# Larger weight loads (18 in place of 22) and three wider transposing matmuls in a single-core decode kernel

## The chip, the cores and the metric

The kernel runs on one core of a Trainium2 chip. The metric is the device time of one execution in microseconds (us). A kernel is run several times, with the kernel before on the same chip beside it; I quote medians. The ratios quoted are the mean time of one kernel's fast runs over that of the other's fast runs of the same rounds, so they are not quite the ratio of the medians; their 95% interval is given in brackets. "Fast" is a label that the measurement gives each run; on one core it marks a run as slow when it lies more than 1.5% above the fastest of the same kernel.

## The reference, cut to what matters

One decode step of a transformer block, batch 2, one token, width 640. There are 32 heads of 192; the last 1,024 rows of the key and value caches count. Everything is bf16.

```python
mod = (silu(c) @ w_mod)                                     # six modulation rows
h = layernorm(x) * (1 + ca) + sa
q = h @ wq                                                  # 640 -> 6144
o = softmax(q k^T * 192**-0.5) v                            # k, v: last 1024 rows of the caches
x = x + ga * (o @ wo)                                       # 6144 -> 640
h = layernorm(x) * (1 + cb) + sb
x = x + gb * ((gelu(h @ w_gate) * (h @ w_up)) @ w_down)     # 640 -> 1536 -> 640
```

Every weight and cache row is read once, 76.88 MB in all, and there are only two tokens to use it on.

## The kernel before

All loads of weights and caches go out from one engine (SP) on one queue, in a fixed order: w_mod, wq, keys and values of batch 0 and 1 interleaved, wo, w_gate, w_up, w_down. They share one arena in the on-chip memory. A load is issued when the tiles that lay in its place have been read. Each load has its own semaphore, so a consumer waits for a whole load, not for the rows that it needs first.

```python
K_SPLIT = [[(0, 64), (64, 64), (128, 128)], [(0, 128), (128, 128)]]   # 5 loads
V_SPLIT = [[(0, 128), (128, 128)], [(0, 128), (128, 128)]]            # 4
WQ_SPLIT = [(0, 2), (2, 3)]                                           # 2
WO_SPLIT = [(0, 28), (28, 17), (45, 3)]                               # 3
WU_SPLIT = [(0, 3), (3, 2)]                                           # 2
WD_SPLIT = [(9, 3), (0, 5), (5, 3), (8, 1)]                           # 4; w_mod and w_gate: one each
# ... cut
def pump(*consumed):                     # issue the next loads whose place is free
    queue["done"].update(consumed)
    while queue["next"] < len(items):
        # ... cut: stop at the first load whose place is still in use
        queue["ops"][it] = S.dma("sp", k_dma(view(it), source(it)), sem_of[it], writes=keys(it), ...)
# ... cut: wo, one group of matmuls for each load
for ci, (t0, n) in enumerate(WO_SPLIT):
    # ... 2 n matmuls, four at a time in four quarters of the array
    S.op("pe", f, reads=keys(("wo", ci)) + ["oT"], ...)
# ... cut: second layer norm, w_gate, gelu, w_up, product aR
def a_T(e):                              # aR (rows in four quarters) to columns
    for i in range(NR):                  # NR = 4
        for r in range(FR):              # FR = 3
            c0 = 2 * (i * FR + r)
            last = e.matmul(ps[:, 2, c0:c0 + B], lhsT=aR[...][:, :, r], rhs=selg[:, i, :], start=True, stop=True)
# ... cut: w_down, one group of matmuls for each load; last product, sum, store
```

## Time and profile before

| | before |
|---|---|
| time, median of 3 runs | 186.31 us (186.27 to 186.47) |
| load queue's share of the 16 DMA engines' span | 97.2% |
| first row moves, last row of w_down has moved | 1.00 us, 181.68 us |
| VectorE busy, TensorE busy | 58%, 58% |

First the DMA lines of the page: the busy share of the 16 DMA engines in 40 slices of the span in tenths, and the load queue with its packets, its MB and its share of the engines' span.

```profile
DMA  9989999999898989999998989899999999999990
...
q1 hardware_dynamic: 3180, 76.88, 97.2%
```

Nines and eights from the first slice to the last but one: the DMA engines never rest. The chain that ended last (start in us, length in us, what) says the same from the other end:

```profile
...
155.23 26.50 DMA arena<-in_B_w_down_dram
181.73 0.04 issue
181.77 0.74 PE ps L690 x16
182.51 0.02 issue
182.54 0.34 DVE fin L695
182.87 0.02 issue
182.89 0.33 DVE finb L697
```

The end of the kernel hangs on w_down's last rows, and then needs 3.3 us: matmuls, two steps on VectorE, and the store. Now the places that the change touches, from the timeline (start, length, engine, line, operation, count; in brackets the idle time before the first of them and what ended it):

```profile
...
21.57 2.73 PE L478 MATMUL ps<-arena,hT 128*2 128x512 bf16 x24 [0.98 <-DVE opc L464]
32.43 4.01 PE L478 MATMUL ps<-arena,hT 128*2 128x512 bf16 x36 [8.13 <-DMA arena<-in_A_wq_dram]
...
40.91 5.09 DVE L504 TENSOR_TENSOR arena<-arena,qbc 128x3072 bf16<-128x3072 bf16 x3 [3.73 <-DMA arena<-in_A_k_cache_dram]
...
62.66 1.76 DVE L504 TENSOR_TENSOR arena<-arena,qbc 128x3072 bf16<-128x3072 bf16 x1 [2.78 <-DMA arena<-in_A_k_cache_dram]
...
160.68 2.08 PE L627 MATMUL ps<-arena,oT 128*2 128x512 bf16 x56 [0.42 <-DMA arena<-in_A_wo_dram]
167.01 1.89 PE L627 MATMUL ps<-arena,oT 128*2 128x512 bf16 x40 [4.25 <-DMA arena<-in_A_wo_dram]
...
174.73 3.64 PE L661 MATMUL ps<-arena,h2T 128*2 128x384 bf16 x40 [0.27 <-DVE h2T L441]
179.11 0.47 PE L678 MATMUL ps<-selg,aR 128*128 128x2 bf16 x12 [0.74 <-DVE aR L670]
...
181.77 0.71 PE L690 MATMUL ps<-arena,aT 128*17 128x160 bf16 x16 [0.62 <-DMA arena<-in_B_w_down_dram]
```

L478 is the wq product: 24 matmuls on the first load, 36 when the second has landed. L504 is the key multiply on VectorE (DVE): it waits for its first key load at 40.91 us and for the third at 62.66 us. L627 is wo, L661 w_gate and w_up, L678 the transpose, L690 w_down.

The trace also has one record for each piece that a DMA engine moves (a row of one partition). Sixteen engines share 128 rows, so a load is eight pieces and one semaphore write on each engine. Mean durations in the kernel before:

```
piece bytes   count   mean ns   16 engines, GB/s
        4       356         9     (semaphore writes)
     1280       128        55     372
     3840       384       152     406
    24576       384       914     430
    49152       896      1821     432
```

### The profile page before, as it was taken

The numbers are of one execution on the slowest core, as the hardware profiler recorded it, in microseconds if no ns is written. First come the engines' busy times: TensorE is split into PE (matmuls) and PEld (weight loads), VectorE is DVE, ScalarE is ACT, GpSimd is POOL, SyncE is SP. The second block draws the span as 40 slices with busy tenths as digits, with TensorE's granted clock in tenths as the row PEclk, the third lists the DMA queues.
The fourth block names the chain that finished last, engine by engine and source line by source line (L and its number), as shares of the span: only waits on it lengthen the run. The fifth ranks groups of instructions, "written<-read, shape, count | busy, mean of one in ns | idle before, by whom it ended". The sixth has DMA issues, their size and how long they took to land.

```text
span 185.0 us, 1611 instructions
## 1 busy us (share of the span) xinstructions
PE 107.2 (58%) x835; PEld 28.5 (15%) x558; DVE 106.7 (58%) x99; ACT 14.5 (8%) x27; POOL 6.5 (4%) x27
## 2 busy tenths in 40 slices
PE   0015720857766379662499565966662499715472
PEld 0011100040000000001252000600001266401231
DVE  6213000119699488965991999789975938202411
ACT  2032100140000000001000000010001000101610
POOL 7600000000000000000000000000000000000000
PEclk9999995555799966998559999999999569996576
DMA  9989999999898989999998989899999999999990
GB/s 324 449 376 436 462 446 404 434 425 494 377 489 361 510 361 489 436 414 457 395 461 383 478 383 489 383 468 436 418 446 404 442 403 449 398 414 426 406 383 34
DMA packets 3202, 76.97 MB, mean 416 GB/s; under 512 B 378, under 2 KB 508, under 8 KB 1148
## 3 DMA queue, kind: packets, MB, share of 16 engines
q1 hardware_dynamic: 3180, 76.88, 97.2%
q8 instruction: 5, 0.08, 0.2%
q10 hardware_dynamic: 16, 0.01, 0.0%
q14 instruction: 1, 0.01, 0.0%
HBM read 76.88 MB, written 0.00 MB: 416 GB/s over the span
## 4 chain that ended last, share of the span: by engine, by line
DMA 57%; DVE 24%; PE 16%; ACT 1%; issue 1%; SPq 1%
DMA arena<-in_A_k_cache_dram 35%; DMA arena<-in_B_w_down_dram 14%; DVE arena L504 14%; PE ps L567 9%; DMA arena<-in_w_mod_dram 8%; DVE S_sb L523 6%; PE ps L516 3%; DVE Em L553 2%; PE ps L456 2%; DVE negm L533 1%; ACT E_sb L541 1%; SPq L283 1%; PE ps L544 1%; PE ps L537 1%; DVE M L529 0%
## 5 line engine op out<-in xcount | busy, mean ns | idle before, releaser
L516 PE MATMUL ps<-arena,ident_b 128*128 128x512 bf16 x192 | 51.3, 412 | 25.8 <-DVE arena L504 25.8
L504 DVE TENSOR_TENSOR arena<-arena,qbc 128x3072 bf16<-128x3072 bf16 x32 | 54.8, 1750 | 8.3 <-DMA arena<-in_A_k_cache_dram 8.3
L567 PE MATMUL ps<-arena,Em 128*64 128x384 bf16 x256 | 26.6, 379 | 5.7 <-DVE Em L553 5.7
L523 DVE TENSOR_REDUCE S_sb<-ps 128x32 f32<-128x1024 f32 x16 | 19.5, 1218 | 10.1 <-PE ps L516 10.1
L567 PEld LDWEIGHTS ps<-arena,Em 128*64 128x64 bf16 x256 | 16.4, 128 | 31.0 <-DVE Em L553 22.2
L553 DVE TENSOR_TENSOR Em<-E_sb,maskE 128x2048 bf16<-128x2048 bf16 x8 | 18.0, 2283 | 3.4 <-PE ps L567 3.4
L478 PE MATMUL ps<-arena,hT 128*2 128x512 bf16 x60 | 6.7, 625 | 9.1 <-DMA arena<-in_A_wq_dram 8.1
L531 PEld LDWEIGHTS ps<-ident_f,M 128*1 128x1 f32 x2 | 0.2, 80 | 60.5 <-DVE M L529 60.5
L488 DVE CAST qrow<-ps 128x512 bf16<-128x512 f32 x1 | 0.7, 692 | 15.0 <-PE ps L478 15.0
L627 PE MATMUL ps<-arena,oT 128*2 128x512 bf16 (+1 forms) x96 | 4.0, 312 | 4.7 <-DMA arena<-in_A_wo_dram 4.7
L635 DVE COPY arena<-ps 128x128 f32<-128x128 f32 x1 | 0.3, 292 | 10.5 <-PE ps L627 10.5
L541 ACT ACTIVATE E_sb<-S_sb,nbias 128x256 bf16<-128x256 f32 x2 | 1.0, 508 | 65.8 <-DVE nbias L539 65.8
L574 ACT ACTIVATE On<-ps,rden 128x384 bf16<-128x384 f32 x2 | 1.2, 580 | 49.5 <-PE ps L567 49.5
L397 PE MATMUL ps<-ident_b,crow 2*128 2x2 bf16 x5 | 0.4, 177 | 7.9 <-DMA crow<-in_c_dram 7.9
L456 PE MATMUL ps<-arena,scT 128*17 128x480 bf16 x40 | 4.3, 597 | 0.7 <-DMA arena<-in_w_mod_dram 0.7
L410 PE MATMUL ps<-st,selstat 128*128 128x2 f32 x4 | 1.1, 348 | 6.1 <-ACT sqj L406 6.1
L402 DVE CAST X<-xr 128x160 f32<-128x160 bf16 x1 | 0.2, 245 | 6.4 <-DMA xr<-in_A_x_dram 6.4
L661 PE MATMUL ps<-arena,h2T 128*2 128x384 bf16 x40 | 3.6, 507 | 0.3 <-DVE h2T L441 0.3
L494 PE MATMUL ps<-qrow,selq 128*128 128x192 bf16 x16 | 2.7, 361 | 1.2 <-ACT qrow L485 1.2
L464 DVE TENSOR_SCALAR opc<-modR 128x160 f32<-128x160 f32 x2 | 0.5, 244 | 4.7 <-ACT modR L461 4.7
L437 PE MATMUL ps<-selrow,hrow 128*32 128x2 bf16 x40 | 0.7, 182 | 3.6 <-DVE hrow L428 3.6
L478 PEld LDWEIGHTS ps<-arena,hT 128*2 128x2 bf16 x20 | 0.6, 107 | 14.3 <-DMA arena<-in_A_wq_dram 9.9
(84 smaller groups left out, 52.8 us busy)
## 6 DMA issues: line engine op xcount, KB each, us to landing
arena<-in_A_v_cache_dram SPq DMA_DIRECT2D x4, 6144.0 KB, 25.8
arena<-in_A_k_cache_dram SPq DMA_DIRECT2D x3, 6144.0 KB, 39.2
arena<-in_A_k_cache_dram SPq DMA_DIRECT2D x2, 3072.0 KB, 42.5
arena<-in_w_mod_dram SPq DMA_DIRECT2D x1, 4800.0 KB, 14.2
arena<-in_A_wq_dram SPq DMA_DIRECT2D x1, 4608.0 KB, 31.2
arena<-in_A_wo_dram SPq DMA_DIRECT2D x1, 4480.0 KB, 25.8
arena<-in_A_wq_dram SPq DMA_DIRECT2D x1, 3072.0 KB, 20.7
arena<-in_A_wo_dram SPq DMA_DIRECT2D x1, 2720.0 KB, 31.9
```

The lines of the kernel that those rows point to most:

```text
L283: return lambda e: e.dma_start(dst, src)
L456: last = e.matmul(ps[32 * i:32 * i + RM, half, 0:MH].rearrange("p (m n) -> p m n", n=DR), lhsT=scT[:, k, :], rhs=wv[:, 3 * half:3 * half + ...
L478: last = e.matmul(ps[32 * i:32 * i + B, n, :], lhsT=hT[:, k, :], rhs=wv[:, kk, i, n * QW:(n + 1) * QW], start=(k == 0), stop=(k == KT - 1) ...
L494: last = e.matmul(ps[:, BK_T + b, 0:Dh], lhsT=selq[:, b, u * P:(u + 1) * P], rhs=qrow[:, u * Dh:(u + 1) * Dh], start=(u == 0), stop=(u == ...
L504: S.op("dve", lambda e: e.tensor_tensor(out=kt, in0=kt, in1=qbc[:, b, :].unsqueeze(1).broadcast_to([P, JC, Dh]), op=ALU.mult), reads=[("qb ...
L516: last = e.matmul(o_ap, lhsT=ident_b[:, :], rhs=kt[:, :, t * GC:(t + 1) * GC], start=(t == 0), stop=(t == NCH - 1))
L523: S.op("dve", lambda e: e.tensor_reduce(out=S_sb[:, b, 2 * JC * pair:2 * JC * (pair + 1)], in_=ps[:, 2 * z:2 * z + 2, :].rearrange("p k (j ...
L541: S.op("act", lambda e: e.activation(out=E_sb[:, b, :], in_=S_sb[:, b, :], func=ACTF.Exp, scale=SCALE, bias=nbias[:, b:b + 1], accum_out=d ...
L553: S.op("dve", lambda e, z=z, j=j: e.tensor_tensor(out=Em[:, z, :, :], in0=E_sb[:, b, j:j + JE].unsqueeze(2).broadcast_to([P, JE, H]), in1= ...
L567: last = e.matmul(ps[64 * i:64 * i + 2 * H, BK_O, 0:ON], lhsT=Em[:, z, 2 * jp:2 * jp + 2, :].rearrange("p j h -> p (j h)"), rhs=view(it, l ...
L627: last = e.matmul(ps[32 * i:32 * i + B, bk, 0:w], lhsT=oT[:, t, :], rhs=wv[:, tl, lo:lo + w], start=(t < NR), stop=(t >= NT - NR), tile_po ...
L661: last = e.matmul(ps[32 * i:32 * i + B, bk, 0:FT].rearrange("p (m r) -> p m r", r=FR), lhsT=h2T[:, k, :], rhs=wk[:, i, :, :], start=(k == ...
```

## The change

The intent is to spend less on the loads themselves: wq and w_up in one load each, wo in two, w_down in three. To make room for the larger wo, tiles move by half a slot. Three matmuls with eight columns replace the twelve with two that transpose the gated activations.

```diff
-    WQ_SPLIT = [(0, 2), (2, 3)]
-    WO_SPLIT = [(0, 28), (28, 17), (45, 3)]
-    WU_SPLIT = [(0, 3), (3, 2)]
-    WD_SPLIT = [(9, 3), (0, 5), (5, 3), (8, 1)]
+    WQ_SPLIT = [(0, KT)]
+    WO_SPLIT = [(0, 39), (39, 9)]
+    WU_SPLIT = [(0, KT)]
+    WD_SPLIT = [(0, 8), (8, 3), (11, 1)]
 ... (cut: places of the tiles in units of half a slot)
-        tiles = [("k", 0, 0, 5), ("k", 0, 1, 6), ("k", 0, 2, 0), ("v", 0, 0, 2), ("k", 1, 0, 4), ...]
+        tiles = [("k", 0, 0, 10), ("k", 0, 1, 12), ("k", 0, 2, 0), ("v", 0, 0, 5), ("k", 1, 0, 9), ...]
-        place[("wo", 0)] = (2 * SLOT, wo_n[0])
-        place[("wo", 1)] = (6 * SLOT, wo_n[1])
-        place[("wo", 2)] = (2 * SLOT + wo_n[0], wo_n[2])
+        place[("wo", 0)] = (4 * HS, wo_n[0])
+        place[("wo", 1)] = (13 * HS, wo_n[1])
 ... (cut)
-            for i in range(NR):
-                for r in range(FR):
-                    c0 = 2 * (i * FR + r)
-                    last = e.matmul(ps[:, 2, c0:c0 + B], lhsT=aR[...][:, :, r], rhs=selg[:, i, :], start=True, stop=True)
+            for r in range(FR):
+                last = e.matmul(ps[:, 2, NR * B * r:NR * B * (r + 1)], lhsT=aR[...][:, :, r],
+                                rhs=selg[:, :, :].rearrange("p i b -> p (i b)"), start=True, stop=True)
```

The change was announced as 18 loads in place of 23. Counted in the code it is 18 in place of 22 (the list above); a load is 128 pieces and 16 semaphore writes, 144 packets.

More of the change, by code (lines that the diff above doesn't have):

```diff
@@ L167, in bass_adaLN_cond__sliding_block_cached__geglu_ffn__decode_kernel @@
     V_SPLIT = [[(0, 128), (128, 128)], [(0, 128), (128, 128)]]
-    assert all(sum(n for _, n in x) == J and all(n % JE == 0 for _, n in x) for x in K_SPLIT + V_SPLIT)
-    WQ_SPLIT = [(0, 2), (2, 3)]
-    WO_SPLIT = [(0, 28), (28, 17), (45, 3)]
-    WU_SPLIT = [(0, 3), (3, 2)]
-    WD_SPLIT = [(9, 3), (0, 5), (5, 3), (8, 1)]
+    assert all(sum(n for _, n in x) == J for x in K_SPLIT + V_SPLIT)
+    assert all(n % (2 * JC) == 0 for x in K_SPLIT for _, n in x) and all(n % JE == 0 for x in V_SPLIT for _, n in x)
+    WQ_SPLIT = [(0, KT)]
+    WO_SPLIT = [(0, 39), (39, 9)]
+    WU_SPLIT = [(0, KT)]
+    WD_SPLIT = [(0, 8), (8, 3), (11, 1)]
     RB = 16
@@ L192, in bass_adaLN_cond__sliding_block_cached__geglu_ffn__decode_kernel @@
         wo_n = [n * D for _, n in WO_SPLIT]
-        place = {("wm", 0): (0, KT * 6 * D), ("wq", 0): (2 * SLOT, wq_n[0]), ("wq", 1): (2 * SLOT + wq_n[0], wq_n[1])}
-        tiles = [("k", 0, 0, 5), ("k", 0, 1, 6), ("k", 0, 2, 0), ("v", 0, 0, 2), ("k", 1, 0, 4), ("v", 0, 1, 0), ("k", 1, 1, 2), ("v", 1, 0, 4), ("v", 1, 1, 0)]
+        HS = SLOT // 2
+        place = {("wm", 0): (0, KT * 6 * D), ("wq", 0): (4 * HS, wq_n[0])}
+        tiles = [("k", 0, 0, 10), ("k", 0, 1, 12), ("k", 0, 2, 0), ("v", 0, 0, 5), ("k", 1, 0, 9), ("v", 0, 1, 0), ("k", 1, 1, 5), ("v", 1, 0, 9), ("v", 1, 1, 0)]
         span = {}
@@ L197, in bass_adaLN_cond__sliding_block_cached__geglu_ffn__decode_kernel @@
             j0, n = (K_SPLIT if kind == "k" else V_SPLIT)[b][t]
-            place[(kind, b, t)] = (z * SLOT, n * Dh)
+            place[(kind, b, t)] = (z * HS, n * Dh)
             span[(kind, b, t)] = (j0, n)
         tiles = [it[:3] for it in tiles]
-        place[("wo", 0)] = (2 * SLOT, wo_n[0])
-        place[("wo", 1)] = (6 * SLOT, wo_n[1])
-        place[("wo", 2)] = (2 * SLOT + wo_n[0], wo_n[2])
-        o_g = 4 * SLOT
+        place[("wo", 0)] = (4 * HS, wo_n[0])
+        place[("wo", 1)] = (13 * HS, wo_n[1])
+        assert 4 * HS + wo_n[0] <= 9 * HS and wo_n[1] <= HS
+        o_g = 9 * HS
         o_u = o_g + KT * F
@@ L674, in a_T @@
             last = None
-            for i in range(NR):
-                for r in range(FR):
-                    c0 = 2 * (i * FR + r)
-                    last = e.matmul(ps[:, 2, c0:c0 + B], lhsT=aR[:, :].rearrange("p (m r) -> p m r", r=FR)[:, :, r], rhs=selg[:, i, :],
-                                    start=True, stop=True)
+            for r in range(FR):
+                last = e.matmul(ps[:, 2, NR * B * r:NR * B * (r + 1)], lhsT=aR[:, :].rearrange("p (m r) -> p m r", r=FR)[:, :, r],
+                                rhs=selg[:, :, :].rearrange("p i b -> p (i b)"), start=True, stop=True)
             return last
         S.op("pe", a_T, reads=["aR", "selg"], writes=[bank(2)], name="aT_T")
-        S.op("dve", lambda e: e.tensor_copy(out=aT[:, :, 0:RM:RB], in_=ps[:, 2, 0:FC * B].rearrange("p (f b) -> p f b", b=B)),
+        S.op("dve", lambda e: e.tensor_copy(out=aT[:, :, 0:RM:RB].rearrange("p (i r) b -> p i r b", r=FR),
+                                            in_=ps[:, 2, 0:FC * B].rearrange("p (r i b) -> p i r b", r=FR, i=NR)),
              reads=[bank(2)], writes=["aT"], name="aT")
```

## The prediction

> **What bounds the kernel now.** The transfers. The page's queue table gives the load queue 97.2% of the sixteen DMA engines' span, 76.88 MB at 416 GB/s. By the trace's DMA records the engines' idle time is within 0.05 us of zero in every 10 us from 10 to 180 us. The chain of waits ends there too: from 155.23 to 181.73 us it is w_down's load, then 0.74 us of matmuls, 0.7 us on VectorE and the store. The time is about 1 us of start, 180.7 us of gapless transfer and 3.3 us of tail.
>
> **What a load costs.** A row piece of 1,280 B takes 55 ns on its engine, one of 49,152 B 1,821 ns (means of the DMA records). A line through the two leaves about 8 ns per piece that does not shrink with size. Each load puts eight pieces and one 9 ns semaphore write on each engine: 73 ns. Five loads fewer are an estimated 0.37 us; the bytes stay. The Trainium skill ("DMA: Bandwidth & Descriptors", Anatomy of one DMA) gives about 2 us fixed per DMA, mostly completion latency. Here it hides behind the next load, whose rows start up to 2 us before the last ones of the load before end, so I do not count 5 x 2 us. The issues saved (0.33 to 0.43 us each on the sync queue) are off the path too.
>
> **What moves.**
> - wq: all its matmuls (2.73 us for the first 24, 4.01 us for the other 36) now start near 32.4 us; q is ready about 2.7 us later. The first key multiply had 1.4 us of slack (q at 39.47, multiply at 40.91), so key work slips about 1.3 us. VectorE then waits 2.78 us for the third key load (62.66 us), which absorbs it.
> - Later issues: the second batch's first key load now overlaps the second key tile: issue near 58 us, not 52.49; first row at 74.8. wo's first: near 136.3, not 134.69; first row at 147.4. w_up: about 154, not 151.7; wanted after 173. No queue runs dry. The tightest issue (second batch's first value load, 114.98 us, first row 118.39) keeps 2 us of margin.
> - wo: the last load, 9 tiles in place of 17 + 3, lands near 168 and needs some 0.85 us of matmuls; the layer norm starts near 168.9 as before.
> - w_up: 20 matmuls wait until 177.4 in place of 8; the product ends about 0.85 us later.
> - Transpose: 3 in place of 12 matmuls, 0.47 us now, an estimated 0.2 us saved.
> - So the down product starts near 180.5, not 179.88. It has 1.63 us of matmuls; the last 16 still wait for the last landing (near 181.4). The tail stays bound by the landing, or overshoots it by up to 0.3 us.
>
> **Sum.** -0.37 us of transfer, 0 to +0.3 in the tail: 186.0 us, range 185.5 to 186.5. Faster by over 2%: 0.01; within 2%: 0.97; slower by over 2%: 0.02.
>
> **What would show it.** Last w_down landing 0.3 to 0.4 us earlier; no idle in the DMA records between 10 and 180 us; VectorE still waiting for the third key load, by about 1.5 us; the wait for w_up larger, the down product's wait for w_down smaller; the chain still through w_down.
>
> **What would make it wrong.** A shift of TensorE's granted clock (0.5 to 1.0 here) that delays buffer releases by over 2 us, so that the queue runs dry near 118 us; or half clock throughout the up product, so that the tail becomes compute-bound and ends 1 us later.

## The result, and the profile after

| | before | after |
|---|---|---|
| time, median of 6 runs each | 186.38 us (186.27 to 186.51) | 185.94 us (185.83 to 186.16) |
| ratio | | 0.9977 [0.9964, 0.9990] |
| last row of w_down has moved | 181.68 us | 181.45 us |

The predicted time was 186.0 us, and the time falls by 0.2%. The predicted range, 185.5 to 186.5 us, also held the time of the kernel before (186.38), so a time inside it says little by itself; the steps have to be checked one by one. The same views of the kernel after, first the page's DMA lines:

```profile
DMA  9999998999798989999898989999998989899980
...
q1 hardware_dynamic: 2604, 76.88, 97.0%
```

The engines are as full as before. The end of the chain:

```profile
...
137.63 26.94 DMA arena<-in_A_wo_dram
164.61 6.31 PE ps L629 x96
...
176.38 3.66 PE ps L663 x34
...
180.75 0.25 PE ps L678 x3
...
181.28 1.04 PE ps L691 x48
...
182.35 0.34 DVE fin L696
```

This is not the chain that was predicted. It leaves the DMA queue at wo's first load, 17 us earlier, and runs on through TensorE, VectorE and ScalarE to the end. The timeline at the same places (the changed kernel's lines are one or two further down: L480, L506, L629, L663, L691):

```profile
...
32.00 6.01 PE L480 MATMUL ps<-arena,hT 128*2 128x512 bf16 x60 [11.81 <-DMA arena<-in_A_wq_dram]
...
40.85 5.09 DVE L506 TENSOR_TENSOR arena<-arena,qbc 128x3072 bf16<-128x3072 bf16 x3 [2.11 <-DMA arena<-in_A_k_cache_dram]
...
62.62 1.76 DVE L506 TENSOR_TENSOR arena<-arena,qbc 128x3072 bf16<-128x3072 bf16 x1 [4.93 <-DMA arena<-in_A_k_cache_dram]
...
164.61 6.27 PE L629 MATMUL ps<-arena,oT 128*2 128x512 bf16 x96 [2.36 <-DMA arena<-in_A_wo_dram]
...
176.38 3.63 PE L663 MATMUL ps<-arena,h2T 128*2 128x384 bf16 x40 [0.28 <-DVE h2T L443]
180.75 0.24 PE L678 MATMUL ps<-selg,aR 128*128 128x8 bf16 x3 [0.74 <-DVE aR L672]
181.28 1.01 PE L691 MATMUL ps<-arena,aT 128*17 128x160 bf16 x48 [0.29 <-DVE aT L682]
```

All 60 matmuls of wq wait for the one load, and yet the first key multiply starts where it did, and VectorE waits longer for the third key load (4.93 us, not 2.78). At wo all 96 matmuls run together after 164.61 us and take 6.27 us, where before 56 had run in 2.08 us while the rest was on its way. The up product no longer waits for a load, and neither does w_down. The clock explains the 6.27 us. The next lines give the stretches (from and to, length, busy time of the engines with the count of instructions, then the granted TensorE clock, where 1.00 is full). First the kernel before while its first wo load is consumed, then the kernel after while it consumes all of wo:

```profile
...
160.00:163.00 3.00, 2.34 (x63) 0.83 (x31) 0.00 (x0) 0.28 (x1) 0.00 (x0) 1.00 0.96 404
```

```profile
...
164.60:171.00 6.40, 6.27 (x96) 1.67 (x48) 0.05 (x1) 0.06 (x1) 0.00 (x0) 0.54 1.02 431
```

The kernel before had the full clock there, the kernel after mostly half of it (0.54). From the end of the value product at 161.06 us to 164.61 us its TensorE had been busy for 0.52 us only; the last 2.36 us of that it waited for the load. The clock record falls to half at 163.60 us, 1 us before wo's first matmul. The Trainium skill ("TensorE: Matmul & The Clock Gate", Part 1) says that the clock is halved by default, that activity releases it, and that activity is judged in free-running windows of about 3.4 us. The clock records of the trace before have only the values 1.0 and 0.5, and their stretches last 3.41, 6.83, 10.24, 13.65, 17.07, 20.48 and 47.79 us, multiples of 3.41 (the last is cut off by the end of the trace).

### The profile page after: what moved, and what is told of

It reads as the page before. It is cut to its first block, busy times and chain, and to the rows that moved or that the text cites. A ratio compares the mean times of both kernels' runs of the same rounds, so it can differ in the third digit from the quotient of the medians.

```text
span 184.8 us, 1589 instructions
## 1 busy us (share of the span) xinstructions
PE 104.6 (57%) x826; PEld 28.5 (15%) x549; DVE 106.7 (58%) x99; ACT 14.5 (8%) x27; POOL 6.5 (4%) x27
## 3 DMA queue, kind: packets, MB, share of 16 engines
q1 hardware_dynamic: 2604, 76.88, 97.0%
HBM read 76.88 MB, written 0.00 MB: 416 GB/s over the span
## 4 chain that ended last, share of the span: by engine, by line
DMA 57%; DVE 20%; PE 19%; ACT 2%; issue 1%; DVEq 0%
DMA arena<-in_A_k_cache_dram 35%; DMA arena<-in_A_wo_dram 15%; DVE arena L506 11%; DMA arena<-in_w_mod_dram 7%; PE ps L518 5%; DVE S_sb L525 4%; PE ps L569 4%; PE ps L629 3%; PE ps L458 2%; PE ps L663 2%; DVE Em L555 1%; ACT L421 1%; PE ps L691 1%; DVE hrow L430 0%; PE ps L439 0%
## 5 line engine op out<-in xcount | busy, mean ns | idle before, releaser
L518 PE MATMUL ps<-arena,ident_b 128*128 128x512 bf16 x192 | 49.1, 399 | 29.0 <-DVE arena L506 29.0
L506 DVE TENSOR_TENSOR arena<-arena,qbc 128x3072 bf16<-128x3072 bf16 x32 | 54.8, 1753 | 9.8 <-DMA arena<-in_A_k_cache_dram 9.8
L480 PE MATMUL ps<-arena,hT 128*2 128x512 bf16 x60 | 6.0, 587 | 11.8 <-DMA arena<-in_A_wq_dram 11.8
L629 PE MATMUL ps<-arena,oT 128*2 128x512 bf16 (+1 forms) x96 | 6.3, 454 | 2.4 <-DMA arena<-in_A_wo_dram 2.4
L663 PE MATMUL ps<-arena,h2T 128*2 128x384 bf16 x40 | 3.6, 507 | 0.3 <-DVE h2T L443 0.3
L480 PEld LDWEIGHTS ps<-arena,hT 128*2 128x2 bf16 x20 | 0.7, 118 | 16.8 <-issue 16.8
L672 DVE TENSOR_TENSOR aR<-ps,gl 128x384 bf16<-128x384 f32 x1 | 0.6, 557 | 3.8 <-PE ps L663 3.8
```

The costliest lines, as they stand in the source:

```text
L480: last = e.matmul(ps[32 * i:32 * i + B, n, :], lhsT=hT[:, k, :], rhs=wv[:, kk, i, n * QW:(n + 1) * QW], start=(k == 0), stop=(k == KT - 1) ...
L506: S.op("dve", lambda e: e.tensor_tensor(out=kt, in0=kt, in1=qbc[:, b, :].unsqueeze(1).broadcast_to([P, JC, Dh]), op=ALU.mult), reads=[("qb ...
L518: last = e.matmul(o_ap, lhsT=ident_b[:, :], rhs=kt[:, :, t * GC:(t + 1) * GC], start=(t == 0), stop=(t == NCH - 1))
L629: last = e.matmul(ps[32 * i:32 * i + B, bk, 0:w], lhsT=oT[:, t, :], rhs=wv[:, tl, lo:lo + w], start=(t < NR), stop=(t >= NT - NR), tile_po ...
L663: last = e.matmul(ps[32 * i:32 * i + B, bk, 0:FT].rearrange("p (m r) -> p m r", r=FR), lhsT=h2T[:, k, :], rhs=wk[:, i, :, :], start=(k == ...
```

## The experiments

**Theory 1.** The gain is engine time of the transfers: each load costs every DMA engine a little, and the engines are the path. **Rival:** the gain is work that left the tail, through the cheaper transposes or the regrouped w_down. **Theory 2**, from the profile after: a load gives its consumer nothing before its last row; merging wo pushed its matmuls together behind a late landing, and this used up the slack between the compute chain and the last transfer. **Theory 3:** the merge of wq was free because VectorE waits for the third key load anyway.

Twelve experiments ran, in three calls (two of them were the changed kernel once more); kernels of one call share their chip and the runs of the kernel before. All gave correct results.

### First call: parts of the change, one at a time

The changed kernel itself, once more:

> The changed kernel once more, unaltered, as the yardstick of its chip. Both theories: 0.9975 to 0.9980 of before, 0.3 to 0.5 us less.

Measured: 186.01 us against 186.13 for before, ratio 0.9993 [0.9980, 1.0005]. That is a smaller gain than in the first comparison and than expected, and its interval includes none. The gain is close to what such a comparison can see. Its profile again shows the chain through wo (96 matmuls in 6.09 us).

Only the transposes, in the kernel before (the edit is the last hunk of the diff above):

> The kernel before with only the three wider transposing matmuls. Theory 1 (the gain is engine time of the transfers, freed by fewer loads): the down product still waits for w_down's last landing, so -0.1 to +0.1 us, ratio 0.9995 to 1.0005. Rival (the gain is work taken out of the tail): about -0.23 us, the time that the transposes lost (0.47 to 0.24 us), or more; ratio 0.9988 or below.

Measured: 186.24 us, ratio 1.0002 [0.9990, 1.0015]. The transposes took 0.24 us in place of 0.47, as expected, and the time did not fall. This speaks for theory 1 against the rival: in this kernel the down product still waited for w_down (12 matmuls from 181.75 us and 4 more at 182.16). The regrouped w_down was not run alone.

Three of the four loads, in the kernel before:

```diff
-    WQ_SPLIT = [(0, 2), (2, 3)]
+    WQ_SPLIT = [(0, KT)]
-    WU_SPLIT = [(0, 3), (3, 2)]
-    WD_SPLIT = [(9, 3), (0, 5), (5, 3), (8, 1)]
+    WU_SPLIT = [(0, KT)]
+    WD_SPLIT = [(0, 8), (8, 3), (11, 1)]
```

> The kernel before with wq and w_up in one load each and w_down in three: three loads fewer (22 to 19), no tile moved, wo in three, transposes in twelve. Theory 1: 3 x 0.07 to 0.10 us = -0.2 to -0.3 us, ratio 0.9984 to 0.9989, last w_down row 0.2 to 0.3 us earlier. Rival (the gain is in the transposes and the moved tiles): within 0.1 us of before.

Measured: 186.05 us, ratio 0.9990 [0.9976, 1.0004]; last w_down row at 181.52 us, 0.16 us earlier than in the profile before. The size is about that of theory 1, but the interval includes no gain: by itself this run settles nothing. Its profile is worth a look, because with wo still in three loads the tail is the one that I had predicted for the whole change: w_up's product waits for its load until 177.37 us, the down product starts at 180.78 us, and the chain runs through w_down.

The changed kernel with twelve transposes again:

> The changed kernel with twelve transposing matmuls again. In the changed kernel's profile the down product no longer waits for a load, the chain runs through wo and TensorE. If that holds in most runs, +0.15 to +0.25 us against the changed kernel of the same call. If the tail is bound by the last landing in most runs (as the prediction had it): within 0.1 us of the changed kernel.

Measured: 186.16 us against 186.01 for the changed kernel of the same call (means 0.10 us apart, single runs of either spread over 0.2 to 0.4 us): inconclusive. In its profile wo's 96 matmuls happened to take 5.11 us, not 6.1 to 6.3, and the chain ran through w_down: the down product started at 180.94 us, 0.34 us earlier than in the changed kernel in spite of the twelve transposes. So which of the two ends last depends, in these profiles, on where the clock's windows fall. And the last row of w_down moved at 181.73 us here, 0.28 us later than in the changed kernel's profile with the same loads: in single profiles the transfers scatter by as much as the change is worth.

### Second call: doubling the suspected cost, and merging too far

Since four loads are hardly visible, I made many. Each of the seven loads of 128 cache rows goes out as four (then eight) loads along its rows, each with a semaphore of its own; the bytes, the places and the consumers stay.

```diff
+                m = PARTS if it in span and span[it][1] == 128 else 1        # PARTS = 4, then 8
+                wid = place[it][1] // m
+                for h in range(m):
+                    ...  S.dma("sp", k_dma(view(it, h * wid, wid), cut(source(it), h * wid, wid, it)), sm,
+                               writes=keys(it, h * wid, wid), ...)
```

> The changed kernel, but each of its seven loads of 128 cache rows goes out as four, along the rows: the same bytes, 21 loads more (39). Theory 1 (every load costs each DMA engine 0.07 to 0.10 us, and the transfers are the path): +1.5 to +2.1 us against the changed kernel, 187.5 to 188.1 us. Fixed cost of about 2 us per load on the path: +40 us. Loads free as long as the queue is full: within 0.2 us.

> As split_free4 with eight parts each: 49 loads more (67). Theory 1: 49/21 of the other's loss, +3.6 to +4.9 us against the changed kernel. If the cost is that of the issue on the sync queue (0.43 us each, hidden while the queue is full), no loss until the issues fall behind the transfers.

Measured: 187.65 us, ratio 1.0068 [1.0056, 1.0080], and 189.69 us, ratio 1.0177 [1.0163, 1.0190], with before at 186.36. The two of them differ by 2.04 us for 28 loads: **0.073 us for a load**, without any other comparison. Against the changed kernel (an estimate: 186.07 us on this chip, from the mean of its three ratios to before, 0.9983) it is 1.59 us for 21 loads and 3.62 us for 49: 0.076 and 0.074 us. The cost is linear and it comes through to the end: the last row of w_down moves at 183.07 and 185.12 us, 1.62 and 3.68 us later than in the changed kernel's profile. This is the line of the load queue with 49 loads more:

```profile
q1 hardware_dynamic: 9660, 76.88, 97.9%
```

It is more packets for the same 76.88 MB, and a higher share of the span, not a lower one: the engines work longer. "Loads free as long as the queue is full" and "2 us each" both fail. In the DMA records, pieces of 12,288 B take 464 ns and of 6,144 B 238 ns; four and eight of them take 35 and 83 ns longer than one of 49,152 B, 12 ns for each piece added. Eight pieces and a semaphore write would then be 105 ns for a load, more than the time shows. The records of pieces overlap a little (in the kernel before they add up to 1.03 of the 16 engines' time from 100 to 121 us); whether that makes the difference is not settled.

All of wo in one load:

```diff
-    WO_SPLIT = [(0, 39), (39, 9)]
+    WO_SPLIT = [(0, 48)]
```

> The changed kernel with wo in one load in place of two: 17 loads. Fewer loads are better, whatever the place: -0.1 us. Theory 2 (a load gives its consumer nothing before its last row, and the chain from wo to the end has almost no slack): all 96 of its matmuls, 4 to 6.3 us, start near 168 us, not 164.6; the tail becomes 2.8 to 3.6 us longer, about 189 us, and the DMA queue stays as full as before.

Measured: 188.61 us, ratio 1.0125 [1.0107, 1.0142]: one load fewer, and 2.5 us slower than the changed kernel's estimate. In its timeline:

```profile
...
168.20 5.35 PE L628 MATMUL ps<-arena,oT 128*2 128x512 bf16 x96 [7.50 <-DMA arena<-in_A_wo_dram]
...
183.96 1.01 PE L690 MATMUL ps<-arena,aT 128*17 128x160 bf16 x48 [0.30 <-DVE aT L681]
```

TensorE waits 7.50 us, begins wo at 168.20 us, and reaches the down product 2.4 us after w_down's last row (181.58 us). Theory 2 holds; the loss came out a little below the range that I had expected.

The first two key loads in one:

```diff
-    K_SPLIT = [[(0, 64), (64, 64), (128, 128)], ...]
+    K_SPLIT = [[(0, 128), (128, 128)], ...]
```

> The changed kernel with the first batch's first two key loads as one: 17 loads. Fewer loads are better, whatever the place: -0.1 us. Theory 3 (what absorbed the wq merge is VectorE's wait of 4.9 us for the third key load): key work starts near 47.7, not 40.85 us, ends near 66, so the third key load (62.6) is taken up 3 to 4.5 us late; each buffer release after it slips so much, and the tightest issue (113.97 us, first row at 118.20) loses its margin of about 2.5 us: idle DMA of 0.5 to 2 us near 119 us, ratio 1.001 to 1.010 against before.

Measured: six runs from 186.08 to 189.60 us, median 188.38. Three of them are labelled slow by the 1.5% rule, which here cuts off the upper half of the scatter, though their granted clock (0.879 to 0.891) is like that of the fast ones (0.877 to 0.902). The fast three give a ratio of 1.0026 [0.9997, 1.0055], so not faster, and the scatter itself is the finding: no other kernel here spreads over 3.5 us. In the one profile there is (of a run labelled slow) key work starts at 47.94 us, as expected, and the tightest issue has slipped from 113.97 to 117.64 us, while the changed kernel moved the first row of that load at 118.20 us; this one moved it at 119.17 us. By the DMA records of that profile, some engines stand idle near 104 us and again from 118 to 122 us (on average 1 to 2 of the 16). So in this run the margin was used up, as theory 3 says; for the fast runs there is no profile. Why its last row then came 3 us late, where the idle time adds up to only 0.55 us of all engines, and why the runs differ so, stays open.

### Third call: another cut of wo, and fewer loads of w_down

The changed kernel for the third time:

> The changed kernel, unaltered, as the yardstick of its chip, for the third time. Four loads fewer at the 0.073 to 0.078 us that the split runs gave: -0.3 us, ratio 0.998 to 0.999. The tail runs through wo and TensorE, not through w_down.

Measured: 185.96 us against 186.31, ratio 0.9980 [0.9968, 0.9992]. With 0.9977 and 0.9993 the mean of the three is 0.9983, 0.31 us; four loads at 0.073 to 0.076 us are 0.29 to 0.30 us. wo took 6.20 us and the tail ran through it.

wo cut more evenly:

```diff
-    WO_SPLIT = [(0, 39), (39, 9)]
+    WO_SPLIT = [(0, 34), (34, 14)]
-        place[("wo", 1)] = (13 * HS, wo_n[1])
+        place[("wo", 1)] = (4 * HS + wo_n[0], wo_n[1])
```

> The changed kernel with wo cut 34 + 14 in place of 39 + 9: the same 18 loads. Theory 2 (39 + 9 bunches all 96 matmuls behind a landing at 164.6 us): the first 68 now start near 162.3 us, the last 28 at 167.6, the layer norm's first step comes 0.5 to 1.5 us earlier, the chain runs through w_down again; 0.1 to 0.2 us less than the changed kernel. If the cut of wo does not matter: within 0.05 us.

Measured: 185.85 us, ratio 0.9977 [0.9964, 0.9989], the lowest of all kernels, but only 0.07 us (means) below the changed kernel of the same call, which is inside the scatter of single runs. The profile is clear where the time is not. The timeline of TensorE, and the first stretch of wo with its clock:

```profile
...
162.61 2.61 PE L629 MATMUL ps<-arena,oT 128*2 128x512 bf16 x68 [0.83 <-DMA arena<-in_A_wo_dram]
167.96 1.25 PE L629 MATMUL ps<-arena,oT 128*2 128x512 bf16 x28 [2.74 <-DMA arena<-in_A_wo_dram]
...
175.04 1.89 PE L663 MATMUL ps<-arena,h2T 128*2 128x384 bf16 x20 [0.28 <-DVE h2T L443]
177.16 1.90 PE L663 MATMUL ps<-arena,h2T 128*2 128x384 bf16 x20 [0.23 <-DMA arena<-in_B_w_up_dram]
...
180.35 0.73 PE L691 MATMUL ps<-arena,aT 128*17 128x160 bf16 x32 [0.31 <-DVE aT L682]
181.42 0.64 PE L691 MATMUL ps<-arena,aT 128*17 128x160 bf16 x16 [0.34 <-DMA arena<-in_B_w_down_dram]
```

```profile
...
162.60:165.30 2.70, 2.61 (x68) 0.88 (x34) 0.00 (x0) 0.00 (x0) 0.00 (x0) 1.00 0.98 418
```

The first part lands 2 us earlier, TensorE waits 0.83 us only, it has the full clock (1.00), and 68 matmuls take 2.61 us. wo ends at 169.2 us in place of 170.9, the waits for w_up and w_down are back, and the last row of w_down sets the end again. So theory 2 holds: in this profile 1.7 us of slack came back, at the same count of loads. The full clock was luck, but the even cut does not need it. In the run with w_down in one load (below), which has the same cut of wo, the first 68 matmuls ran at a clock of 0.65 and were still done before the second load came:

```profile
...
162.91 3.89 PE L629 MATMUL ps<-arena,oT 128*2 128x512 bf16 x68 [2.19 <-DMA arena<-in_A_wo_dram]
168.12 1.25 PE L629 MATMUL ps<-arena,oT 128*2 128x512 bf16 x28 [1.31 <-DMA arena<-in_A_wo_dram]
...
```

That the slack is worth little in time says how little the changed kernel's tail overshot: its last four matmuls began at 182.06 us; by the lag of 0.48 us that other runs show between the last row's end and the start of its matmuls, they could have begun at 181.93 us.

w_down in two loads, then in one (both with the even cut of wo):

```diff
-    WD_SPLIT = [(0, 8), (8, 3), (11, 1)]
+    WD_SPLIT = [(0, 8), (8, 4)]          # then [(0, FC)]
-        stop=(fc == WD_SPLIT[-1][0])
+        stop=(fc == FC - 1)
```

> As a_wobal, with w_down in two loads (8 + 4 rows): 17 loads. In every profile bound by the landing, the last 16 matmuls ran together after it, so the cut of the last row buys nothing: one load less, 0.07 us less than a_wobal, 0.2 to 0.3 us less than the changed kernel.

> As a_wobal, with w_down in one load: 16 loads, 0.15 us less of transfer, but all 48 matmuls (1.0 to 1.6 us) behind the last landing in place of the last 16 (0.65 us): +0.4 to +0.9 us against a_wobal_wd2. Fewer loads are better whatever the place: -0.07 us against it.

Measured: 186.06 us, ratio 0.9989 [0.9977, 1.0001], and 187.11 us, ratio 1.0041 [1.0023, 1.0058]. The first expectation was a miss: one load fewer came out 0.2 us slower. I had read the 16 matmuls at the end of the timeline as one wait. The chain splits them:

```profile
...
181.42 0.39 PE ps L691 x12
181.81 0.01 issue
181.81 0.28 PE ps L691 x4
...
```

```profile
...
181.80 0.48 PE ps L691 x16
...
```

With three loads, 12 matmuls run at 181.42 us on the second load, and only 4 at 181.81 us on the third. With two loads, all 16 start at 181.80 us. The last load of one row saves what the 12 cost, more than its 0.073 us. With w_down in one load, 48 matmuls wait until 181.96 us and take 1.78 us at half the clock (0.50):

```profile
...
181.96 1.78 PE L691 MATMUL ps<-arena,aT 128*17 128x160 bf16 x48 [1.78 <-DMA arena<-in_B_w_down_dram]
```

The clock record had fallen to half at 181.13 us. By the medians this is 1.05 us slower than two loads (single runs 186.55 to 187.52 us), a little over what I had expected, and again "fewer loads" loses. The clock is partly luck: with the same cut of wo, the first 68 matmuls took 2.61 us in one run and 3.89 us in this one.

## Why the prediction was right, point by point

- **What bounds the kernel: right.** The DMA engines, gapless. The split runs show that loads added to their queue appear in the time, in proportion to their number.
- **The cost of a load: right in size.** 73 ns, from a line through two piece sizes; the split runs gave 73 to 76 ns. How it comes about is not shown: the smaller pieces of the split runs would make it 105 ns by the same reckoning, so the close agreement is partly luck.
- **The count: wrong.** "Five loads fewer are an estimated 0.37 us" took the count from the announcement. There are four fewer: 0.29 us. The mean of three comparisons is 0.31 us; in the profiles the last row of w_down moved 0.23 us earlier, where 0.3 to 0.4 us had been announced. The sum still fell into the range because this step was off by 0.07 us only.
- **"so I do not count 5 x 2 us": right.** 49 loads more cost 3.6 us, not 98. (The page's figure is for loads issued from GpSimd, which the prediction did not say; these are issued from the sync engine.)
- **wq, "key work slips about 1.3 us", absorbed by the third key load: absorbed, but there was no slip.** TensorE had more of its full clock there (60 matmuls in 6.01 us, where before 24 and 36 took 2.73 and 4.01 us; the 16 of the next product in 1.48 us, not 2.72), so the first half of q was ready at 40.43 us, 1.0 us later than before and not 2.7, and the key load itself still came last (40.85 us). The early merge of two key loads suggests that this room is finite.
- **"Later issues", "No queue runs dry": right.** The tightest issue went out at 113.97 us and its first row moved at 118.20 us. w_up went out at 155.90 us, 2 us later than announced, since the value product before it ran later; it still landed before it was wanted.
- **"the layer norm starts near 168.9 as before": wrong, the failed step.** It starts with wo's evacuation, at 170.94 us. I had costed the last load's 18 matmuls only and had not asked when the first load's 78 could run, nor that TensorE would come out of a wait at half clock. By an estimate it took both: at the rate of the kernel before (56 in 2.08 us) the 78 would have been done near 167.5 us, before the second load, whose last row moved at 167.57 us, and the layer norm would have started near 168.7 us. At half clock the merged load left no room; the three loads before, and the even cut, did. In all three profiles of the changed kernel the clock fell to half between 163.2 and 163.7 us; in the run with twelve transposes, at 165.88 us.
- **"the wait for w_up larger", "the chain still through w_down": wrong, from the same step.** The compute chain was 2 us late, so every load was there when it was asked for. The down product started at 181.28 us, not 180.5, and took 1.01 us, not 1.63, since it waited for nothing and had the full clock.
- **The tail "overshoots it by up to 0.3 us": right in size**, about 0.13 us by the estimate above; but for another reason than the one given (w_up), so this is luck.
- **The transposes: right.** 0.24 us in place of 0.47, and nothing of it in the time while the tail waits for a transfer.

## What to carry to other kernels

Where the transfers are gapless, a load more or less was worth little here (73 ns for 128 rows), so merging loads pays only where no consumer needs the first part early. Before merging, ask of each load when its consumer could start on the first part, how much slack its chain has to the end, and whether the consumer comes out of its wait at a lower clock: merging wo fully cost 2.5 us and merging w_down fully 1.05 us, to save 0.07 each. And count the loads in the code and in the packets of the queue, not in a description.

## What the Trainium skill lacked or had wrong

- "DMA: Bandwidth & Descriptors", Anatomy of one DMA: it gives about 2 us fixed for a DMA (its fit is for loads issued from GpSimd). It lacks what a load costs in a full queue issued from the sync engine: 0.073 to 0.076 us for 128 rows.
- The same page, the same section, says that most of the fixed cost is the receipt after the last byte. That is said of loads issued from GpSimd. Here, issued from the sync engine, the matmuls began 0.48 us after the last row of w_down had moved (181.32 to 181.80 us, w_down in two loads), much less than most of 2 us; whether a row's record already includes some of the receipt, no run here shows.
- The same page, Latency and other measured facts: about 0.6 us to the first byte for loads issued from the sync engine. It does not say from where this is counted. Here the first row of the first load moved 1.00 us after its issuing instruction began, and 0.62 us after that instruction (0.38 us) ended, which agrees with the page.
- The same page, Bandwidth: it says that for loads from HBM the HBM side (about 358 GB/s for a core) binds; the same section limits this to both cores of a pair streaming, and gives 425 GB/s as measured for 16 MB on one core. One core alone moved 416 GB/s over the span, and 16 x 61,440 B in 2,268 ns are 433 GB/s.
- The same page, Rules for kernel authors: one large transfer in place of many small ones. It is a rule for small transfers (it names 64 KB) and does not cover the merging of large ones: wo in one load of 7.86 MB was 2.5 us slower than in two, because its consumer could not start on the first part.
- "TensorE: Matmul & The Clock Gate", Part 1: values and window agree with the clock records here. It says that one idle window of about 3.4 us brings the half clock; here the stretch need not be idle throughout: in the 3.41 us before the clock record fell to half at 163.60 us (changed kernel), TensorE was busy for 1.39 us, and in the 3.41 us before it fell at 181.13 us (w_down in one load), for 1.72 us. No fixed share comes out of the traces: 1.47 us of such a stretch (161.29 to 164.70 us, kernel before) left the clock full.
